# A three-stage kernel (attention, expert layer, dense layer): q with exchanged halves by TensorE and VectorE, not by DMA; two small operations on other engines

## The chip, the cores and the metric

The program runs on one core of one Trainium2 chip. The metric is the device time in microseconds from one launch to the end. Three runs of the kernel before gave 1102.35, 1104.45 and 1104.64 us, median 1104.45. A core has TensorE (PE; its weight loads stand apart as PEld), VectorE (DVE), ScalarE (ACT), GpSimd (POOL) and SyncE (SP), which issues most of the DMAs; 16 DMA engines move the data.

## The reference

Attention with a threshold on 4 batches x 8 heads, 576 positions, width 64; its output feeds a layer of 8 experts (top 1), and that a dense layer with `h - tanh(h)`. All in float32. Only the attention bears on the change:

```python
scores = scale * np.matmul(q, k.transpose(0, 1, 3, 2))
thresh = np.max(scores, axis=-1, keepdims=True) - tau
scores = np.where(scores >= thresh, scores, -1000000000.0)
scores = scores - np.max(scores, axis=-1, keepdims=True)
attn = np.exp(scores)
attn = attn / (np.sum(attn, axis=-1, keepdims=True) + 1e-09)
return np.matmul(attn, v).astype(np.float32)
```

## The kernel before

The attention is cut into 16 units. A unit is one head of two batches (`j` = 0, 1), and its 1152 rows of q are worked off in nine steps `t` of 128 rows; step 4 takes 64 rows of each batch. Partitions 0 to 63 and 64 to 127 hold the two halves of a float32 split: of q and k the rounded part (`hi`, by ScalarE, `split_hi`) and the rest (`lo`, `split_lo`), put side by side in the tile `x2`, transposed by TensorE (`tr`: the pieces `q0`, `m`, `q4`, `k0`, `k5`) into the one PSUM tile with the tag `t`, and written from there to SBUF (`evac`). So `QA` ("qa", 128 x 1280, of which 1216 columns are used) has q's rounded part on the partitions of one half and its rest on the other. The scores need all four products of parts, and get them as two products of full depth: `QA` with `ka`, and `QB` ("qb") with `ka`, where `QB` is `QA` with the two halves of its partitions exchanged. Two DMAs per unit make it (`swap`, L192 to L195), issued by SP.

What a step then does, engine by engine: TensorE writes the scores to PSUM (`scores`, L213, three buffers); VectorE takes the negative maximum (`smax`, L221); ScalarE the exponential (`sexp`, L227); VectorE masks, multiplies and sums (`smask`, L240, the sum into a column of `su`), and makes the next threshold (`sthr`, L231); ScalarE rounds the result to float16 (`split_e`, L248, tile `e16` with three buffers of three steps each); GpSimd makes the rest (`split_l`, L252 and L253). After three steps SP issues a DMA transpose of `e16` into `et` (`tr_e`, L259), and TensorE multiplies `et` by the two float16 parts of v (`pv`, L282). VectorE scales the products by the reciprocal `r` of the sums while it writes them to `x` (`pv_out`, L288). The reciprocal is made by `recip`: VectorE adds 1e-9 to `su` and multiplies it by v's scale `sc` (L267), then inverts it (L268). v itself is multiplied by its scale on VectorE (`v_w`, L137), rounded on ScalarE (`v_hi`, L141), and its rest is made on GpSimd (`v_lo`, L145). v's maximum (`v_max`, L123) is the first thing that uses a load of v (`load_v`, L103 to L105).

Each engine works off its instructions in the order in which the program is written. That order comes from a table: in `PL` each job has a pair (step, slot), relative to the first step of its unit; `PFIRST` and `PLAST` replace entries for the first and the last unit; `AFTER` lists which job has to stand ahead of which. `run` walks through the steps of all units: slot 0, the scores of the step after the next, slot 1, the maximum and exponential of the next step, the mask of this step, the next threshold, slots 2 and 3. A unit lasts nine steps, so the jobs of one unit's inputs lie among the steps of the unit before. After the last step come the routing to the experts, the expert layer and the dense layer; the change does not touch them.

The first unit's exchange is made in two pieces (`swap0` and `swap`).

Of the kernel before, what the change touches and what calls it, by code (L numbers as in the profile page):

```python
# [11 lines left out]
F32 = mybir.dt.float32  # L12
F32R = mybir.dt.float32r
# [4 lines left out]
AF = mybir.ActivationFunctionType  # L18
ALU = mybir.AluOpType
# [4 lines left out]
B, H, S, D = 4, 8, 576, 64  # L24
# [3 lines left out]
QS = S + 64  # L28


class Attn:
# [3 lines left out]
    def __init__(self, tc, ctx, q, k, v, tau, xtok, ident):  # L35
        self.tc, self.nc = tc, tc.nc
        self.q, self.k, self.v = q, k, v
        self.xtok, self.ident = xtok, ident
        nc = self.nc
        e = ctx.enter_context  # L40
        self.one = e(tc.tile_pool(name="a1", bufs=1))
        self.ld = e(tc.tile_pool(name="ald", bufs=2))
        self.wk = e(tc.tile_pool(name="awk", bufs=2))
        self.sp = e(tc.tile_pool(name="asp", bufs=3, space=PSUM))
        self.tp = e(tc.tile_pool(name="atp", bufs=1, space=PSUM))
        one = self.one
        self.raw, self.x2, self.vv, self.vs, self.vh, self.ka = {}, {}, {}, {}, {}, {}
        self.X, self.rr, self.rqk, self.tpu = {}, {}, {}, {}
        w = one.tile([128, 1], F32, name="warm")
        nc.vector.memset(w, 0.0)  # L50
        nc.scalar.activation(out=w, in_=w, func=AF.Exp)
        t = one.tile([128, 1], F32, name="tau")
        nc.gpsimd.dma_start(out=t, in_=tau.to_broadcast([128, 1]))
        self.load_qk(0, 0, 0, 1, nc.sync)
        self.load_qk(0, 1, 0, 1, nc.scalar)
        self.identr = one.tile([128, 128], F32R, name="identr")
        nc.vector.tensor_copy(self.identr, ident)
        self.g8 = one.tile([128, 1], F32, name="g8")
        nc.vector.tensor_scalar(out=self.g8, in0=t, scalar1=0.0, scalar2=0.125, op0=ALU.is_ge, op1=ALU.mult)
        self.ntau = one.tile([128, 1], F32, name="ntau")  # L60
        nc.vector.tensor_scalar(out=self.ntau, in0=t, scalar1=0.0, scalar2=-1.0, op0=ALU.max, op1=ALU.mult)
        z = one.tile([128, 64], F32, name="z64")
        nc.gpsimd.memset(z, 0.0)
        self.QA, self.QB = [], []
        for i in range(2):
            for lst, nm in ((self.QA, "qa"), (self.QB, "qb")):
                tl = one.tile([128, 2 * QS], F32R, name=f"{nm}{i}")
                nc.vector.tensor_copy(tl[:, S:S + 64], z)
                lst.append(tl)
        bank = self.tp.tile([128, 512], F32, name="ops")  # L70
        self.ops = bank[:, 0:6 * D].rearrange("p (a b d) -> p a b d", a=2, b=3)
        w = 6 * D + 9 * H
        self.lm = bank[:, 6 * D:w].rearrange("p (t e) -> p t e", t=9)
        self.vsum = bank[:, w:w + 4]
        self.c14 = one.tile([128, 128], F32, name="c14")
        nc.gpsimd.memset(self.c14, 2.0 ** -14)
        self.em, self.e16, self.et, self.sums = {}, {}, {}, {}
# [56 lines left out]
        V.reciprocal(out=sc, in_=pm)  # L134

    def v_w(self, u):
        self.nc.vector.tensor_scalar(out=self.vv[u], in0=self.vv[u], scalar1=self.vs[u][1], scalar2=None, op0=ALU.mult)  # L137

    def v_hi(self, u):
        self.vh[u] = self.wk.tile([128, 2, 2, 5, D], F16, tag="vh", name="vh", bufs=2)  # L140
# [51 lines left out]
    def swap(self, u, c0=0, c1=QS + S):  # L192
        a, bq = self.QA[u % 2].bitcast(F32), self.QB[u % 2].bitcast(F32)
        for o in (0, 64):
            self.nc.sync.dma_start(out=bq[o:o + 64, c0:c1], in_=a[64 - o:128 - o, c0:c1])  # L195


    def scores(self, u, t):
        nc = self.nc
        ps = self.sp.tile([128, 2, 512], F32, tag="s", name="sps")  # L200
        qa, qb, ka = self.QA[u % 2], self.QB[u % 2], self.ka[u]
        if t == 4:
            terms = [(j, 512 + 64 * j) for j in range(2)]
        elif t < 4:
            terms = [(0, 128 * t)]
        else:
            terms = [(1, QS + 64 + 128 * (t - 5))]
        n = len(terms) * 2
        i = 0
        for w in (qa, qb):  # L210
            for j, o in terms:
                for c in range(2):
                    nc.tensor.matmul(ps[:, c, 0:288], lhsT=w[:, o:o + 128], rhs=ka[:, j, 288 * c:288 * c + 288],  # L213
                                     start=(i == 0), stop=(i == n - 1))
                i += 1
        return ps
# [43 lines left out]
        self.et[u, g] = et  # L260


    def recip(self, u):
        nc = self.nc
        su = self.sums.pop(u)
        r = self.wk.tile([128, 9], F32, tag="r", name="r")
        nc.vector.tensor_scalar(out=su, in0=su, scalar1=1e-9, scalar2=self.vs[u][1], op0=ALU.add, op1=ALU.mult)  # L267
        nc.vector.reciprocal(out=r, in_=su)  # L268
        self.rr[u] = r

    def pv(self, u, t):
# [19 lines left out]
    def store(self, u):  # L291
        nc = self.nc
        P, h = divmod(u, H)
        if h % 2 == 1:
            c = slice((h - 1) * D, (h + 1) * D)
            X = self.X[u // 2]
            for j in range(2):
# [7 lines left out]
    PL = {"lq": (-21, 1), "lk": (-31, 2), "lv": (-12, 1), "hi0": (-16, 2), "hi1": (-15, 3), "lo0": (-13, 1),  # L305
# [6 lines left out]

    PFIRST = {"hi0": (-20, 2), "hi1": (-18, 0), "lo0": (-18, 0), "lo1": (-18, 1), "q0": (-17, 0), "eq0": (-16, 2),
# [6 lines left out]

    AFTER = ["lq hi0", "lk hi1", "hi0 lo0", "hi1 lo1", "lo0 q0", "lo0 q4", "lo0 m", "lo1 m", "lo1 k0", "lo1 k5", "q0 eq0",
             "eq0 m", "m em", "em q4", "q4 eq4", "eq4 k0", "k0 ek0", "ek0 k5", "k5 ek5", "eq0 swap", "em swap", "eq4 swap", "vm vn", "vn vc", "vc vw", "vw vh", "vh vl", "se sl", "sl te", "po2 st",
             "po0 t0", "po1 t1", "po2 t2", "t0 v0", "v0 t1", "t1 v1", "v1 t2", "t2 v2", "v0 l0", "v1 l1", "v2 l2", "l0 la", "l1 la", "l2 la"]

    def run(self, units, moe=None):
        nc = self.nc
# [3 lines left out]
        for x in self.AFTER:  # L330
            x, y = x.split()
            assert PL[x] < PL[y] or PL[x] == PL[y] and list(PL).index(x) < list(PL).index(y), (x, y)

        def at(b, job, f, *a):
            i, ph = PL[job]
            sched.setdefault((b + i, ph), []).append((f, a))

        for n, u in enumerate(units):
            b = 9 * n
            PL = {**self.PL, **(self.PFIRST if n == 0 else self.PLAST if n == NU - 1 else {})}  # L340
            if n % 4 == 0:
                e0 = 0 if n else 1
                at(b, "lq", self.load_qk, u // 4, 0, e0, 4)
                at(b, "lk", self.load_qk, u // 4, 1, e0, 4)
                at(b, "lv", self.load_v, u // 4)
                for e in range(4):
                    at(b + e, "vm", self.v_max, u + e)
                at(b, "vn", self.v_sum, u)
                at(b, "vc", self.v_scale, u)
            for i in range(2):  # L350
                at(b, f"hi{i}", self.split_hi, u, i)
            for i in range(2):
                at(b, f"lo{i}", self.split_lo, u, i)
            for w in ("q0", "m", "q4", "k0", "k5"):
                at(b, w, self.tr, u, w)
                at(b, "e" + w, self.evac, u, w)
            if n == 0:
                at(b, "swap0", self.swap, u, 0, 256)
            at(b, "swap", self.swap, u, 256 if n == 0 else 0)
            at(b, "vw", self.v_w, u)  # L360
            at(b, "vh", self.v_hi, u)
            at(b, "vl", self.v_lo, u)
            for t in range(9):
                at(b + t, "se", self.split_e, u, t)
                if n == NU - 1:
                    at(b + t, "se", self.split_l, u, t // 3, slice(t % 3, t % 3 + 1), nc.vector if t in self.LD else nc.gpsimd)
                elif t % 3:
                    at(b + t, "sl", self.split_l, u, t // 3, slice(2 * (t % 3 - 1), t % 3 + 1), nc.gpsimd)
                if t % 3 == 2:
                    at(b + t - 2, "te", self.tr_e, u, t // 3)  # L370
                at(b + t, "pv", self.pv, u, t)
            for g in range(3):
                at(b, f"po{g}", self.pv_out, u, g)
            at(b, "rc", self.recip, u)
            at(b, "st", self.store, u)
            if moe and u % 2 == 1:
                P, j = u // H, u % H // 2
                for g in range(3):
                    at(b, f"t{g}", moe.lg_tr, P, j, g)
                    at(b, f"v{g}", moe.lg_ev, P, j, g)  # L380
                    at(b, f"l{g}", moe.lg_mm, P, j, g)
                at(b, "la", moe.lg_add, P, j)
# [942 lines left out]
```

## Time and profile before

| | us |
|---|---|
| runs, median (lowest to highest) | 1104.45 (1102.35 to 1104.64) |
| the profiled execution | 1109.76 |
| its span, first to last instruction | 1108.1 |
| PE busy | 950.4 (86%) |
| DVE busy | 904.0 (82%) |
| POOL busy | 727.1 (66%) |
| ACT busy | 663.3 (60%) |

Busy times are of the whole span, and the stages differ: the attention lies between some 11 and 376 us after the start, the expert layer and the dense layer behind it. A share of DMA can pass 1, since a DMA engine can have more than one packet under way. A wait is written `engine what it was about to do <- who ended the wait`. A trailing `q` (SPq) is an engine's sequencer, which issues DMAs.

### The profile page before, as it was taken

Reading aid. Unit: us, or ns where it says so; the run is one execution under the profiler, and the core shown is the slowest. Engines: PE = TensorE matmul, PEld = TensorE weight load, DVE = VectorE, ACT = ScalarE, POOL = GpSimd, SP = SyncE. Lnnn points to the kernel's source line nnn. Section 1 sums busy time; section 2 is a strip of 40 time slices with the busy share of each in tenths; the row PEclk is TensorE's granted clock in tenths of the full one; section 3 lists DMA queues with packets and bytes.
Section 4 is the critical chain, followed back from the end, with each engine's and each line's share of the span. In section 5 each row is a group of like instructions: output and inputs, shape, how many; then the busy total and the mean of one; then the engine's idle time right before and its main releaser. Section 6 shows DMA issues by size and latency. Waiting matters only on the chain.

```text
span 1108.1 us, 20727 instructions
## 1 busy us (share of the span) xinstructions
PE 950.4 (86%) x7297; PEld 875.3 (79%) x7297; DVE 904.0 (82%) x1605; ACT 663.3 (60%) x1246; POOL 727.1 (66%) x629
## 2 busy tenths in 40 slices
PE   4687686875877557999999989899999999999997
PEld 3576675864766447989999989788999999999886
DVE  4898876966979449897789875998988989899894
ACT  5686776965887134444455546676566665656662
POOL 2886875865777236544466646887767767677673
PEclk9687886977898769899999999999999999999999
DMA  6899999999999766687888876420100101000000
GB/s 178 169 206 191 195 196 215 197 192 204 165 200 182 135 207 234 218 275 246 258 265 282 272 256 217 132 86 17 34 22 20 46 11 41 16 29 1 20 10 29
DMA packets 249769, 162.51 MB, mean 147 GB/s; under 512 B 180122, under 2 KB 222508, under 8 KB 249661
## 3 DMA queue, kind: packets, MB, share of 16 engines
q1 hardware_dynamic: 245901, 150.36, 57.1%
q0 software_dynamic: 3312, 10.49, 2.8%
q8 instruction: 59, 0.97, 0.4%
q14 instruction: 49, 0.40, 0.1%
q10 hardware_dynamic: 448, 0.30, 0.1%
HBM read 85.08 MB, written 23.60 MB: 98 GB/s over the span
## 4 chain that ended last, share of the span: by engine, by line
PE 46%; DVE 11%; issue 3%; DMA 2%; ACT 2%; POOL 1%; POOLq 0%; SPq 0%; DVEq 0%; ACTq 0%
PE h L1008 23%; PE y L1091 15%; PE y L1063 8%; DVE w L1204 2%; DVE w L1205 2%; DVE w L978 1%; DMA raw<-in_moe_w_dram 1%; DVE cv L1125 1%; DVE w L1202 1%; PE t L985 1%; DMA xr<-rows,idx 1%; ACT w L976 1%; DVE cm L1123 1%; DVE tm L1203 1%; DVE w L1206 1%
## 5 line engine op out<-in xcount | busy, mean ns | idle before, releaser
L252 POOL TENSOR_TENSOR e<-em,e 128x1024 f16<-128x1024 f32 (+1 forms) x98 | 158.3, 1615 | 88.2 <-ACT e L248 59.5
L1201 POOL TENSOR_SCALAR tm<-u 128x384 uint8<-128x384 f32 x88 | 128.7, 1463 | 50.5 <-ACT u L1197 49.9
L1008 PE MATMUL h<-xa,w 128*128 128x256 f32 (+6 forms) x864 | 139.8, 311 | 8.8 <-DVE hbuf L1044 6.6
L1063 PE MATMUL y<-hbuf,w 128*128 128x256 f32 (+6 forms) x864 | 139.8, 311 | 0.7 <-ACT yo L1066 0.7
L1008 PEld LDWEIGHTS h<-xa,w 128*128 128x128 f32 x864 | 129.8, 193 | 11.2 <-DVE hbuf L1044 7.7
L227 ACT ACTIVATE e<-sps,n 128x576 f32<-128x576 f32 x144 | 108.1, 751 | 49.8 <-DVE n L221 49.2
L240 DVE SCALAR_TENSOR_TENSOR em<-sps,n,e 128x576 f32<-128x576 f32 x144 | 116.5, 809 | 24.3 <-ACT e L227 17.3
L978 POOL TENSOR_TENSOR w<-raw,w 128x1024 fp32r<-128x1024 f32 x36 | 92.3, 2563 | 58.8 <-ACT w L976 38.7
L282 PE MATMUL ops<-vh,et 128*128 128x64 f16 (+1 forms) x2240 | 102.0, 206 | 32.5 <-DVE x L288 29.1
L1063 PEld LDWEIGHTS y<-hbuf,w 128*128 128x128 f32 x864 | 127.7, 191 | 1.4 <-ACT yo L1066 0.9
L221 DVE TENSOR_REDUCE n<-sps 128x1 f32<-128x576 f32 x144 | 107.1, 744 | 23.3 <-PE sps L213 23.2
L282 PEld LDWEIGHTS <-et 128*128 128x128 f16 (+1 forms) x2240 | 89.0, 111 | 44.8 <-issue 34.7
L1204 DVE SCALAR_TENSOR_TENSOR w<-y,w 128x384 f32<-128x384 f32 x96 | 123.7, 1289 | 0.0
L1197 ACT ACTIVATE u<-h 128x384 f32<-128x384 f32 x96 | 47.1, 491 | 118.6 <-PE h L1008 118.6
L248 ACT CAST e<-em 128x576 f16<-128x576 f32 x144 | 97.3, 677 | 31.6 <-DMA et<-e 30.3
L213 PE MATMUL sps<-ka,qa 128*128 128x288 f32 x320 | 91.3, 380 | 28.6 <-DVE em L240 23.2
L1008 PE MATMUL h<-xk,w 128*128 128x384 f32 x576 | 109.4, 337 | 2.0 <-DVE w L978 1.7
L1218 POOL TENSOR_TENSOR gl<-w,gh 128x384 fp32r<-128x384 f32 x83 | 85.2, 1027 | 38.8 <-ACT gh L1217 38.8
L1008 PEld LDWEIGHTS h<-xk,w 128*128 128x128 f32 x576 | 102.1, 188 | 6.7 <-DVE w L978 2.4
L1043 ACT ACTIVATE hbuf<-h 128x256 fp32r<-128x256 f32 (+6 forms) x72 | 31.1, 432 | 108.4 <-PE h L1008 108.3
L976 ACT CAST w<-raw 128x1024 fp32r<-128x1024 f32 x72 | 75.3, 1050 | 21.8 <-DVE poff L576 14.7
L1205 DVE SCALAR_TENSOR_TENSOR w<-y,w 128x384 f32<-128x384 f32 x96 | 77.3, 805 | 10.7 <-DVE w L1204 0.9
(224 smaller groups left out, 2264.7 us busy)
## 6 DMA issues: line engine op xcount, KB each, us to landing
raw<-in_moe_w_dram SPq DMA_DIRECT2D x64, 512.0 KB, 5.0
qb<-qa SPq DMA_DIRECT2D x30, 304.0 KB, 5.7
cv<-in_moe_w_in_dram SPq DMA_DIRECT2D x16, 512.0 KB, 6.3
cv<-in_moe_w_out_dram SPq DMA_DIRECT2D x16, 512.0 KB, 4.7
wscr<-cm SPq DMA_DIRECT2D x32, 256.0 KB, 2.4
raw<-wscr SPq DMA_DIRECT2D x16, 512.0 KB, 4.3
xw<-yT SPq DMA_DIRECT2D x24, 192.0 KB, 2.4
vv<-in_v_dram SPq DMA_DIRECT2D x8, 512.0 KB
```

Of the source, the lines that this page charges most:

```text
L221: nc.vector.tensor_reduce(out=n[:, 0:1], in_=ps[:, :, 0:288], axis=AX.XY, op=ALU.max, negate=True)
L227: nc.scalar.activation(out=e, in_=ps[:, :, 0:288], func=AF.Exp, bias=n[:, 0:1])
L240: nc.vector.scalar_tensor_tensor(out=self.em[u, g][:, i].rearrange("p (a b) -> p a b", a=2), in0=ps[:, :, 0:288], scalar=n[:, 1:2], in1=e, ...
L252: eng.tensor_tensor(out=e16[:, r, S + 64:], in0=em[:, r, 0:512], in1=e16[:, r, 0:512], op=ALU.subtract)
L282: nc.tensor.matmul(o[q], lhsT=et[:, base + c, q], rhs=vh[:, a, j, c if c < 5 else c - 5, :], start=(n == 0), stop=(n == len(terms) - 1))
L978: (self.nc.gpsimd if pool else self.nc.vector).tensor_tensor(out=l, in0=raw, in1=h.bitcast(F32), op=ALU.subtract)
L1008: self.nc.tensor.matmul(out, lhsT=a, rhs=b, start=(i == 0), stop=(i == len(parts) - 1))
L1063: nc.tensor.matmul(self.ys[d], lhsT=a[:, f % 2, s], rhs=b, start=(f == 0 and i == 0), stop=(f == 7 and i == 2))
L1091: nc.tensor.matmul(self.ys[m], lhsT=a[:, s], rhs=b[:, f % 2], start=(f == 0 and i == 0), stop=(f == 15 and i == 2))
L1201: nc.gpsimd.tensor_scalar(out=mk, in0=u, scalar1=RCUT * RCUT, scalar2=None, op0=ALU.is_gt)
L1204: V.scalar_tensor_tensor(out=w, in0=y, scalar=b, in1=w, op0=ALU.add, op1=ALU.mult)
L1205: V.scalar_tensor_tensor(out=w, in0=z, scalar=d, in1=w, op0=ALU.add, op1=ALU.mult)
```

## The change

From the second unit on, `QB` is no longer written by DMA. A constant 128 x 128 tile `flip` is the identity with its two column halves exchanged. `turn` multiplies it on TensorE with a third of `QA` (512, 512 and 192 columns) into the PSUM tile with the tag `t`, of which there is one buffer, shared with the transposes `tr` and with the expert layer's `lps`; `turned` copies that on VectorE to `QB`. The jobs are s0, x0, s1, x1, s2, x2 in this order. The first unit keeps its DMAs. Besides, the first half of `recip` becomes a job of its own on GpSimd (`denom`), four steps ahead of the rest, and `v_w` is an activation on ScalarE in place of the operation on VectorE. `PL` has seven new entries (a line of them is shown), `AFTER` the order "de rc", "em s0", "eq4 s0", and the chain s0 to x2.

```diff
         nc.vector.tensor_copy(self.identr, ident)
+        self.flip = one.tile([128, 128], F32R, name="flip")
+        for o in (0, 64):
+            nc.vector.tensor_copy(self.flip[:, o:o + 64], ident[:, 64 - o:128 - o])
...
     def v_w(self, u):
-        self.nc.vector.tensor_scalar(out=self.vv[u], in0=self.vv[u], scalar1=self.vs[u][1], scalar2=None, op0=ALU.mult)
+        self.nc.scalar.activation(out=self.vv[u], in_=self.vv[u], func=AF.Copy, scale=self.vs[u][1])
...
+    def turn(self, u, i):
+        self.tps = self.tp.tile([128, 4, 128], F32R, tag="t", name="tws")
+        a = self.QA[u % 2][:, 512 * i:min(512 * i + 512, QS + S)]
+        self.nc.tensor.matmul(self.tps.rearrange("p a b -> p (a b)")[:, 0:a.shape[1]].bitcast(F32), lhsT=self.flip, rhs=a,
+                              start=True, stop=True)
+
+    def turned(self, u, i):
+        b = self.QB[u % 2][:, 512 * i:min(512 * i + 512, QS + S)]
+        self.nc.vector.tensor_copy(b, self.tps.rearrange("p a b -> p (a b)")[:, 0:b.shape[1]].bitcast(F32))
...
+    def denom(self, u):
+        su = self.sums[u]
+        self.nc.gpsimd.tensor_scalar(out=su, in0=su, scalar1=1e-9, scalar2=self.vs[u][1], op0=ALU.add, op1=ALU.mult)
+
     def recip(self, u):
         nc = self.nc
-        su = self.sums.pop(u)
         r = self.wk.tile([128, 9], F32, tag="r", name="r")
-        nc.vector.tensor_scalar(out=su, in0=su, scalar1=1e-9, scalar2=self.vs[u][1], op0=ALU.add, op1=ALU.mult)
-        nc.vector.reciprocal(out=r, in_=su)
+        nc.vector.reciprocal(out=r, in_=self.sums.pop(u))
         self.rr[u] = r
...
+          "s0": (-7, 2), "x0": (-7, 3), "s1": (-6, 1), "x1": (-6, 2), "s2": (-6, 3), "x2": (-6, 3),
...
-            at(b, "swap", self.swap, u, 256 if n == 0 else 0)
+                at(b, "swap", self.swap, u, 256)
+            else:
+                for i in range(3):
+                    at(b, f"s{i}", self.turn, u, i)
+                    at(b, f"x{i}", self.turned, u, i)
...
+            at(b, "de", self.denom, u)
             at(b, "rc", self.recip, u)
```

What this makes of the order. First SP's queue in the middle of the attention, where `e_` tiles are `e16` and `raw` and `qb` the inputs; before:

```order
L259 DMA_TRANSPOSE et<-e_1621 128x27x128
L195 DMA qb_110<-qa_108 64x1216 x2
L259 DMA_TRANSPOSE et<-e_1749 128x27x128
L259 DMA_TRANSPOSE et<-e_1851 128x27x128
L90 DMA raw<-in_q_dram 64x4x576 x2
L259 DMA_TRANSPOSE et<-e_1956 128x27x128
L195 DMA qb_114<-qa_112 64x1216 x2
```

and now:

```order
L272 DMA_TRANSPOSE et<-e_1659 128x27x128
L272 DMA_TRANSPOSE et<-e_1787 128x27x128
L272 DMA_TRANSPOSE et<-e_1888 128x27x128
L93 DMA raw<-in_q_dram 64x4x576 x2
L272 DMA_TRANSPOSE et<-e_2001 128x27x128
```

The two exchange DMAs that stood behind the first of a unit's three transposes are gone, and nothing takes their place in this queue. Second VectorE, in the steps in which the inputs of the next unit are made (L288, now L303, is `pv_out`); before:

```order
L288 TENSOR_TENSOR x<-ops,r 128x3x64 x2
L221 TENSOR_REDUCE n<-sps 128x1
L240 SCALAR_TENSOR_TENSOR em,su<-sps,n,e 128x576
L231 TENSOR_SCALAR n<-n,ntau 128x1
L267 TENSOR_SCALAR su<-su,sc 128x9
L268 RECIPROCAL r<-su 128x9
L221 TENSOR_REDUCE n<-sps 128x1
L240 SCALAR_TENSOR_TENSOR em,su<-sps,n,e 128x576
L231 TENSOR_SCALAR n<-n,ntau 128x1
L137 TENSOR_SCALAR vv<-vv,sc 128x2x320
```

and now, from the same `pv_out` on:

```order
L303 TENSOR_TENSOR x<-ops,r 128x3x64 x2
L209 CAST qb_113<-tws 128x512
L234 TENSOR_REDUCE n<-sps 128x1
L253 SCALAR_TENSOR_TENSOR em,su<-sps,n,e 128x576
L244 TENSOR_SCALAR n<-n,ntau 128x1
L209 CAST qb_113<-tws 128x512
L209 CAST qb_113<-tws 128x192
L283 RECIPROCAL r<-su 128x9
```

The operations on `su` and on `vv` have left VectorE; three copies from the PSUM tile `tws` stand there instead, the second and the third with nothing between them. Third TensorE, where the transposes of k follow (`k0`, `k5`); before:

```order
L282 MATMUL ops<-vh,et 128x64
L164 MATMUL tps<-identr,x_1883 128x128 x4
L213 MATMUL sps<-ka,qa_108 128x288 x2
L213 MATMUL sps<-ka,qb_110 128x288 x2
L536 MATMUL ops<-wg,xT 128x8 x3
L164 MATMUL tps<-identr,x_1883 128x128 x4
```

and now:

```order
L297 MATMUL ops<-vh,et 128x64
L204 MATMUL tws<-qa_115,flip 128x192
L167 MATMUL tps<-identr,x_1922 128x128 x4
L226 MATMUL sps<-ka,qa_111 128x288 x2
L226 MATMUL sps<-ka,qb_113 128x288 x2
L557 MATMUL ops<-wg,xT 128x8 x3
L167 MATMUL tps<-identr,x_1922 128x128 x4
```

The last of the three products stands directly ahead of the transposes of k and of the scores, in the same PSUM tile as those transposes. On GpSimd the operation on `su` stands between the two parts of the last group's rests (L252, L253), ahead of the single step's.

## Rows read from the trace of the kernel before

**Rows 1.** The page's share of the DMA engines, in 40 slices of the span

```profile
DMA  6899999999999766687888876420100101000000
```

**Rows 2.** Busy time of each engine by stretch, clock, DMA share and rate

```profile
core 0: us, PE busy (x) PEld busy (x) DVE busy (x) ACT busy (x) POOL busy (x), PEclk, DMA share, GB/s
11.00:376.00 365.00, 267.32 (x3361) 241.95 (x3360) 287.60 (x723) 258.47 (x449) 258.03 (x286) 0.83 1.06 192
...
60.00:340.00 280.00, 206.86 (x2700) 189.53 (x2699) 226.61 (x566) 207.42 (x363) 202.65 (x192) 0.84 1.10 194
...
182.00:185.00 3.00, 2.64 (x22) 2.13 (x22) 2.97 (x5) 1.84 (x4) 2.58 (x3) 0.50 0.98 187
...
180.90:199.30 18.40, 14.68 (x171) 13.32 (x172) 18.00 (x43) 14.18 (x26) 12.09 (x12) 0.67 1.03 180
```

**Rows 3.** DMA in 60 to 340 us: packets, and the exchange's issues

```profile
DMA packets 150244, 54.40 MB, mean 194 GB/s; under 512 B 136184, under 2 KB 147064, under 8 KB 150210
...
qb<-qa SPq DMA_DIRECT2D x26, 304.0 KB, 5.7
```

**Rows 4.** Waits in 60 to 340 us: who waited for whom, total, times, longest

```profile
ACT e L248 <- DMA et<-e: 28.6, 12, 4.4
...
DVE em L240 <- ACT e L227: 17.3, 8, 4.1
...
DVE n L221 <- PE sps L213: 15.9, 24, 1.9
...
DVE pm L123 <- DMA vv<-in_v_dram: 12.9, 3, 4.7
...
PE sps L213 <- DMA qb<-qa: 0.4, 1, 0.4
```

**Rows 5.** Waits of SP's DMA queue in 60 to 340 us

```profile
SPq L259 <- POOL e L253: 83.4, 23, 7.4
```

**Rows 6.** Instructions in order of time: start, duration, engine, operation, idle before it

```profile
155.40 1.18 SPq L195 DMA_DIRECT2D qb<-qa  x2
156.69 11.85 SPq L259 DMA_TRANSPOSE et<-e  x2
...
167.00 0.67 ACT L248 CAST e<-em 128x576 f16<-128x576 f32 x1 [3.43 <-DMA et<-e]
...
168.98 0.82 DVE L240 SCALAR_TENSOR_TENSOR em<-sps,n,e 128x576 f32<-128x576 f32 x1 [2.99 <-ACT e L227]
...
179.46 0.82 DVE L123 TENSOR_REDUCE pm<-vv 128x1 f32<-128x640 f32 x1 [4.69 <-DMA vv<-in_v_dram]
...
198.76 0.42 POOL L253 TENSOR_TENSOR e<-em,e 128x128 f16<-128x128 f32 x1
...
202.49 1.33 DVE L267 TENSOR_SCALAR su<-su,sc 128x9 f32<-128x9 f32 x1
```

**Rows 7.** Groups by line and shape: count, busy us and mean ns of one

```profile
L1091 PE MATMUL y<-w,gh 128*128 128x512 f32 x258 | 81.1, 395 | 1.9 <-POOL w L978 1.1 <-ACT gh L1217 0.4 <-ACT yw L1066 0.3
...
L267 DVE TENSOR_SCALAR su<-su,sc 128x9 f32<-128x9 f32 x16 | 16.1, 1004 | 0.0
L288 DVE TENSOR_TENSOR x<-ops,r 128x192 f32<-128x192 f32 x48 | 15.4, 347 | 10.5 <-PE ops L282 10.5
L137 DVE TENSOR_SCALAR vv<-vv,sc 128x640 f32<-128x640 f32 x16 | 14.1, 882 | 0.0
...
L141 ACT CAST vh<-vv 128x640 f16<-128x640 f32 x16 | 11.6, 728 | 0.0
...
L188 DVE CAST ka<-two 128x512 fp32r<-128x512 f32 x1 | 0.7, 692 | 0.2 <-PE two L164 0.2
```

**Rows 8.** Single lines: durations in ns, lowest, median and highest

```profile
L137 DVE TENSOR_SCALAR vv<-vv,sc x16: 541/546/1818, 39.9 to 354.3; 128x640 f32<-128x640 f32 x16
...
L267 DVE TENSOR_SCALAR su<-su,sc x16: 227/1140/1658, 49.0 to 363.6; 128x9 f32<-128x9 f32 x16
...
L240 DVE SCALAR_TENSOR_TENSOR em<-sps,n,e x144: 800/808/820, 19.2 to 362.8; 128x576 f32<-128x576 f32 x144
```

More of the change, by code (lines that the diff above doesn't have):

```diff
@@ L322 @@
              "eq0 m", "m em", "em q4", "q4 eq4", "eq4 k0", "k0 ek0", "ek0 k5", "k5 ek5", "eq0 swap", "em swap", "eq4 swap", "vm vn", "vn vc", "vc vw", "vw vh", "vh vl", "se sl", "sl te", "po2 st",
-             "po0 t0", "po1 t1", "po2 t2", "t0 v0", "v0 t1", "t1 v1", "v1 t2", "t2 v2", "v0 l0", "v1 l1", "v2 l2", "l0 la", "l1 la", "l2 la"]
+             "po0 t0", "po1 t1", "po2 t2", "t0 v0", "v0 t1", "t1 v1", "v1 t2", "t2 v2", "v0 l0", "v1 l1", "v2 l2", "l0 la", "l1 la", "l2 la", "de rc", "em s0", "eq4 s0", "s0 x0", "x0 s1", "s1 x1", "x1 s2", "s2 x2"]
     def run(self, units, moe=None):
```

2 rows, old and new, of the table PL are left out of this document.

## The prediction

> **What bounds the kernel now.** I read the profile's slices first. The DMA engines are at nine tenths and over in most of the first third and nearly idle at the end [rows 1], so the stages have different limits. The change lies wholly in the attention; I take the stages after it as they are. From 11 to 376 us the DMA share is 1.06 [rows 2], above 1 because packets overlap. In the steady part, 60 to 340 us, it is 1.10, at 194 GB/s [rows 2]. That stretch holds 26 exchange DMAs [rows 3], two per unit, so 13 units, 280 / 13 = 21.5 us each. Per unit VectorE is busy 226.6 / 13 = 17.4 us, ScalarE 16.0, TensorE 15.9, GpSimd 15.6 [rows 2]. No engine fills the unit; DMA does.
>
> The waits tell how this reaches the engines. ScalarE waits 28.6 us for a transpose to free the float16 buffer, twelve times; VectorE 17.3 us for ScalarE; VectorE 12.9 us for v [rows 4]. In order of time one sees one such wait whole: the exchange's DMAs are issued at 155.40, the transposes behind them take SP 11.85 us for two, ScalarE's cast at 167.00 has waited 3.43 us for a transpose, and VectorE's mask at 168.98 another 2.99 us for ScalarE [rows 6]. The exchanged q itself is nearly never late (0.4 us, once) [rows 4]: it costs bandwidth, not latency.
>
> **The change part by part.** *DMA removed.* In 60 to 340 us the exchange carries 26 x 304 KB = 8.09 MB of 54.40 [rows 3], 14.9%. At the stretch's rate that is 0.149 x 280 = 41.6 us, 3.2 us a unit. A stretch that is nearly all exchange says the same: 0.623 MB a pair at 187 GB/s is 3.3 us [rows 2]. The unit's floor by DMA falls from 21.5 to 18.3 us. Fifteen units lose their exchange, the first keeps it: at most 15 x 3.2 = 48 us. SP also loses its two issues, 1.18 us a unit [rows 6]; what stood behind them is a transpose, which moves up.
>
> *VectorE.* Away go the scaling of v, 14.1 / 16 = 0.88 us, and the operation on the sums, 16.1 / 16 = 1.01 us [rows 7]. In come three copies out of PSUM. The row that fits is the 128x512 cast out of PSUM into the same type, 0.692 us [rows 7]; for 192 columns I take the 128x192 row, 0.347 us [rows 7]. Sum 1.73, net -0.16 us a unit.
>
> Both removed operations swing: 0.541 to 1.818 us for v's scaling, 0.227 to 1.658 us for 9 columns of sums, while the mask, L240, stays within 800 to 820 ns [rows 8]. So some 0.34 + 0.78 us of the two is waiting, inside the instruction. If it passes to another VectorE operation, the net is 1.73 - 0.54 - 0.23 = +0.96 us instead. I take -0.16, since the commonest operation that stays shows no such swing, and keep +0.96 in the range. The Trainium skill, SBUF — State Buffer, "Who interferes with whom", says VectorE and GpSimd share a port pair that is locked for a whole instruction, taken by VectorE's copies and scalings within SBUF, not by an operation with at most one input there. The mask's even row agrees; by that rule the waits leave with the two operations, and the sum is -0.16. Against the change speaks VectorE: DVE Perf Modes, "Mode 2×_2P": float32 scalings within SBUF run at double rate, reads out of PSUM do not. The trace agrees (640 columns in 546 ns, 512 out of PSUM in 692); by that alone the sum would be +0.96.
>
> *Added waits between TensorE and VectorE.* One PSUM buffer serves all three products, so each product waits for the copy before it. The first two hand-offs have a maximum and a mask (some 1.5 us) between them; nothing stands between the second copy and the third, so VectorE waits there for a whole product. No row shows this. Below, it is nothing, if VectorE has other waits in the same place. A 128x512 product takes 0.395 us at full clock [rows 7], 0.8 at 1.2 GHz (clock 0.50 occurs in this stage [rows 2]). If all five hand-offs are in series, they cost 3 x 0.4 + 1.73 = 2.9 us, of which the copies are counted: 1.2 us, 2.4 at half clock. Queued behind VectorE's wait is the reciprocal and the next maximum, for which ScalarE waits; behind TensorE's are the transposes of k and the next scores. In every second unit the first product also waits for ScalarE to empty the buffer of the router's transposes. I take 0.8 us, nearer to a product than to the series.
>
> *TensorE's* own work grows by at most 3 x 0.395 = 1.2 us a unit, 2.4 at half clock, on 15.9. *ScalarE* gets v's scaling: the row of its 640-column cast, 0.73 us [rows 7], on 16.0; the cast waited for this scaling anyway. *GpSimd* gets nine columns: above by its 128x128 row, 0.42 us, below by nothing. These three stay at or under 18.3 and are hidden by DMA and VectorE; uncovered they would cost up to 2.4, 0.7 and 0.4 us a unit. *The reciprocal* now waits for GpSimd. In the unit shown GpSimd has ended the operation ahead at 199.2 and VectorE comes to the sums at 202.49 [rows 6], 3.3 us of slack. Nothing; if it fails, the next maximum stands behind.
>
> *The sum.* What is late next is VectorE: 17.4 - 0.16 + 0.8. To that come waits that DMA does not cause: for the scores, 15.9 / 13 = 1.2 us; and half of v's waits, 12.9 / 13 / 2 = 0.5 us, since v's transfer is long itself and VectorE's arrival moves forward too. Together 19.75 us, over DMA's 18.3. The unit gets 1.75 us shorter, times 15 = 26 us. The profiled execution would go from 1109.76 (span 1108.1 and 1.7 around it) to 1084. The median of the runs is 5.3 us (0.5%) lower; taking 26 off it gives 1078.
>
> **The rivals.**
> *A: DMA sets the pace throughout.* All transfers stay dense and the whole 48 us come back: 1056. For it: the share of 1.10. Against it: SP waits 83.4 us of the 280 for GpSimd's float16 rests [rows 5], so the queue is not always fed; and from 180.9 to 199.3 VectorE is busy 18.0 of 18.4 us [rows 2], so it has no 3.2 us to give.
> *B: hidden anyway.* The chain VectorE, ScalarE, GpSimd, transpose sets the pace, and the time that the exchange gives back becomes idle DMA. For it: the same two rows. Against it: the 3.43 and 2.99 us waits right behind an exchange [rows 6]. Time: the net of VectorE, -0.16 to +0.96 a unit, with up to 0.5 us back from shorter waits: 1097 to 1112, about 1103.
> *C: slower, by the one PSUM buffer.* TensorE, in order, holds the scores back behind each copy; VectorE then waits for scores as well as products. Price: all hand-offs in series at half clock, 2.4 us a unit, plus one product that the scores wait for, 0.8, plus VectorE's +0.96. It decides from the point where this sum passes what DMA gives back, 3.2 us: 4.2 - 3.2 = 1.0 us a unit, 15 us: 1119. Against it: the first two hand-offs have other work between them, and the scores are made two steps ahead.
> That the change doesn't remove the DMAs is excluded: the transposes now stand next to each other in SP's queue.
>
> **How the numbers follow.** Chances: forecast 0.58, A 0.18, B 0.14, C 0.10. The forecast's own range is 1066 (no added waits: 0.8 us a unit, 12 us more) to 1095 (+0.96 in place of -0.16: 1.1 us a unit, 17 us less). The range of 8 in 10 takes in half of A and the better half of B: 1056 to 1101. Runs of this kernel lie 0.2% apart (2.3 us), so less than that is no change. Faster: 0.58 + 0.18 and 0.07 of B, 0.83. Same: 0.04, of B. Slower: 0.10 and 0.03 of B, 0.13.
>
> **What would show it.** Right: four exchange DMAs in the trace (the first unit's) where there were 34; ScalarE's wait for transposes well under 28.6 us in 13 units; units of 19 to 20 us; copies near 0.69 us; VectorE over 88% busy in the steady part, DMA share below 1.05. Waits of VectorE for products under 1 us a unit; L267's swing gone and L240 still within 800 to 820 ns. Wrong: the unit still at 21 us with idle DMA (B); waits of TensorE for the copies and of VectorE for the products above 2 us a unit (C); VectorE's other operations growing by the 1.1 us that the two removed ones waited; the reciprocal waiting for GpSimd.

## The result, and the profile after

The changed kernel takes 1079.89 us (median of 4 runs, 1077.72 to 1083.33), the kernel before 1103.84 us beside it (4 runs, 1102.35 to 1104.64). The ratio is 0.9776 with a 95% interval of 0.9752 to 0.9799: faster by 2.2%, 24 us. The forecast was 1078. The two profiled executions differ by more, 1109.76 against 1077.72, since the one of before lies above its other runs and the one of after is the lowest of its own.

The page after, with the span, the busy shares and the DMA slices (to hold against [rows 1]):

```profile
span 1075.6 us, 20756 instructions
...
PE 949.5 (88%) x7342; PEld 870.1 (81%) x7342; DVE 898.7 (84%) x1620; ACT 670.6 (62%) x1262; POOL 728.5 (68%) x645
...
DMA  6798999998989476786787976220100101000000
```

The attention is over about a slice sooner; the rest looks as it did. From the last mask (VectorE's operation that ends a step's work on the scores; L240 before, L253 after) to the end of the span it is 745.3 us before and 744.9 after, so all of the gain lies in the attention. Between the two profiled executions that is 32 us, between the medians 24, or 1.6 us for each of the fifteen units. In the steady part, which is 60 to 320 us here, the windows show (microseconds; busy time and count of each engine; TensorE's granted clock; DMA share; GB/s):

```profile
core 0: us, PE busy (x) PEld busy (x) DVE busy (x) ACT busy (x) POOL busy (x), PEclk, DMA share, GB/s
60.00:320.00 260.00, 213.65 (x2826) 190.50 (x2825) 230.71 (x600) 218.90 (x385) 211.65 (x212) 0.92 0.99 186
...
216.20:234.60 18.40, 16.99 (x223) 15.40 (x223) 16.71 (x46) 16.57 (x30) 15.41 (x15) 0.91 1.21 200
234.60:260.50 25.90, 17.87 (x212) 15.79 (x211) 20.24 (x52) 17.03 (x32) 16.93 (x18) 0.80 0.88 178
260.50:278.80 18.30, 16.90 (x224) 15.48 (x223) 16.56 (x45) 16.47 (x31) 15.56 (x15) 0.91 0.99 178
```

Against [rows 2] the DMA share falls from 1.10 to 0.99 and VectorE rises from 226.6 of 280 (81%) to 230.7 of 260 (89%). The lower three rows are three units in a row. Units 2 to 15, from first mask to first mask, take (315.1 - 41.1) / 14 = 19.6 us on average, before (346.2 - 42.6) / 14 = 21.7. They are of two kinds: the three that load v (the middle row is one) take 22.4 to 25.9 us, before 26.4 to 27.5; the other eleven 18.4 on average, before 20.2. In the plain unit of the last row VectorE is busy 16.6 of 18.3 us. TensorE's mean granted clock is higher too, 0.92 after against 0.84 in [rows 2].

The waits in 60 to 320 us (engine and line that waited, whom for; total, times, longest):

```profile
ACT e L240 <- DVE n L234: 24.7, 19, 7.0
...
PE tws L204 <- DVE qb L209: 20.9, 16, 5.8
...
DVE pm L126 <- DMA vv<-in_v_dram: 10.9, 3, 5.6
...
DVE qb L209 <- PE tws L204: 8.2, 16, 0.6
PE ops L297 <- DVE x L303: 7.2, 11, 0.9
...
DVE n L234 <- PE sps L226: 5.1, 12, 0.6
```

ScalarE's wait for the transposes, which led [rows 4], has no row any more. ScalarE and TensorE now wait for VectorE, and VectorE for v, for the products (L204, copied at L209) and, less than before, for the scores (L226). The groups of the added work (count | busy, mean ns | idle before):

```profile
L209 DVE CAST qb<-tws 128x512 fp32r<-128x512 f32 x30 | 20.5, 684 | 4.3 <-PE tws L204 4.2
...
L140 ACT ACTIVATE vv<-vv,sc 128x640 f32<-128x640 f32 x16 | 13.4, 836 | 0.0
...
L209 DVE CAST qb<-tws 128x192 fp32r<-128x192 f32 x15 | 5.3, 356 | 4.9 <-PE tws L204 4.9
L278 POOL TENSOR_SCALAR su<-su,sc 128x9 f32<-128x9 f32 x16 | 4.4, 274 | 1.6
```

### The profile page after: what moved, and what is told of

It reads as the page before. It is cut to its first block, busy times and chain, and to the rows that moved or that the text cites. A ratio compares the mean times of both kernels' runs of the same rounds, so it can differ in the third digit from the quotient of the medians.

```text
span 1075.6 us, 20756 instructions
## 1 busy us (share of the span) xinstructions
PE 949.5 (88%) x7342; PEld 870.1 (81%) x7342; DVE 898.7 (84%) x1620; ACT 670.6 (62%) x1262; POOL 728.5 (68%) x645
## 4 chain that ended last, share of the span: by engine, by line
PE 50%; DVE 8%; DMA 3%; issue 3%; ACT 1%; POOL 1%; POOLq 0%; DVEq 0%; SPq 0%; ACTq 0%; another core or an unknown queue 0%
PE h L1029 25%; PE y L1112 15%; PE y L1084 9%; DVE w L1225 2%; DVE w L1226 1%; DMA xr<-rows,idx 1%; PE t L1006 1%; DMA raw<-in_moe_w_dram 1%; DVE w L1223 1%; DVE cv L1146 1%; DVE w L999 1%; DVE tm L1224 1%; DVE w L1227 0%; DVE cm L1148 0%; ACT w L997 0%
## 5 line engine op out<-in xcount | busy, mean ns | idle before, releaser
L240 ACT ACTIVATE e<-sps,n 128x576 f32<-128x576 f32 x144 | 110.9, 770 | 33.1 <-DVE n L234 32.9
L253 DVE SCALAR_TENSOR_TENSOR em<-sps,n,e 128x576 f32<-128x576 f32 x144 | 116.7, 811 | 5.3 <-ACT e L240 3.4
L234 DVE TENSOR_REDUCE n<-sps 128x1 f32<-128x576 f32 x144 | 107.2, 744 | 10.6 <-PE sps L226 10.5
L297 PE MATMUL ops<-vh,et 128*128 128x64 f16 (+1 forms) x2240 | 95.8, 200 | 13.8 <-DVE x L303 12.9
L297 PEld LDWEIGHTS <-et 128*128 128x128 f16 (+1 forms) x2240 | 82.2, 106 | 25.8 <-issue 20.9
L261 ACT CAST e<-em 128x576 f16<-128x576 f32 x144 | 100.4, 698 | 2.0 <-DVE em L253 1.5
L226 PE MATMUL sps<-ka,qa 128*128 128x288 f32 x320 | 86.2, 362 | 9.4 <-DVE em L253 5.4
```

The costliest lines, as they stand in the source:

```text
L234: nc.vector.tensor_reduce(out=n[:, 0:1], in_=ps[:, :, 0:288], axis=AX.XY, op=ALU.max, negate=True)
L240: nc.scalar.activation(out=e, in_=ps[:, :, 0:288], func=AF.Exp, bias=n[:, 0:1])
L253: nc.vector.scalar_tensor_tensor(out=self.em[u, g][:, i].rearrange("p (a b) -> p a b", a=2), in0=ps[:, :, 0:288], scalar=n[:, 1:2], in1=e, ...
L261: self.nc.scalar.copy(self.e16[u, g][:, i, 0:S], self.em[u, g][:, i])
L297: nc.tensor.matmul(o[q], lhsT=et[:, base + c, q], rhs=vh[:, a, j, c if c < 5 else c - 5, :], start=(n == 0), stop=(n == len(terms) - 1))
```

## The experiments

Four runs took the change apart: the product alone, the two moves alone, and the change with the exchange's traffic or only its issues put back.

**The product alone.** The scaling of v and the operation on the sums go back to VectorE; the exchange stays on TensorE.

```diff
-        self.nc.scalar.activation(out=self.vv[u], in_=self.vv[u], func=AF.Copy, scale=self.vs[u][1])
+        self.nc.vector.tensor_scalar(out=self.vv[u], in0=self.vv[u], scalar1=self.vs[u][1], scalar2=None, op0=ALU.mult)
...
-        self.nc.gpsimd.tensor_scalar(out=su, in0=su, scalar1=1e-9, scalar2=self.vs[u][1], op0=ALU.add, op1=ALU.mult)
...
+        nc.vector.tensor_scalar(out=su, in0=su, scalar1=1e-9, scalar2=self.vs[u][1], op0=ALU.add, op1=ALU.mult)
```

> The exchange by product and copies, as in the changed kernel; v's scaling and the operation on the sums back on VectorE. Two limits (mine): with the exchange gone VectorE sets the pace, so its 1.9 us a unit of removed work come back nearly whole: 15 x 1.2 to 1.9 us = 18 to 28 us over the changed kernel, 1098 to 1108, about no gain over before. DMA alone: VectorE has slack, so 1080 as changed, at most 1085. VectorE's relief alone: copies added and nothing taken away, so slower than before, 1115 or more.

1099.0 us, ratio 0.994 (0.9914 to 0.9966): a quarter of the gain. The DMA share is down to 0.92, and VectorE, busy 236.7 of 260 us (91%), is the nearer limit:

```profile
60.00:320.00 260.00, 206.09 (x2649) 183.93 (x2648) 236.71 (x579) 200.54 (x350) 195.12 (x185) 0.90 0.92 173
```

**The moves alone.** The scaling on ScalarE and the sums on GpSimd, as in the change, with the exchange by DMA as before.

```diff
-                for i in range(3):
-                    at(b, f"s{i}", self.turn, u, i)
-                    at(b, f"x{i}", self.turned, u, i)
+                at(b, "swap", self.swap, u, 0)
```

> v's scaling on ScalarE and the operation on the sums on GpSimd, as in the changed kernel; the exchange by DMA as before. Two limits (mine): the DMA engines go on setting the pace, VectorE's 1.9 us a unit are mostly idle time: 1096 to 1104. DMA alone: 1104, no change. VectorE's relief alone: 15 x 1.9 = 28 us faster, 1076, or more, since no copies are added.

1104.18 us, ratio 0.9987 (0.9965 to 1.0009): no difference. VectorE is relieved, from 211.6 to 193.0 us in these 260, and DMA keeps the pace. ScalarE still waits for the transposes (25.0 us before in the same stretch), and VectorE's waits for ScalarE grow from 14.1 us, so its relief turns into waiting:

```profile
60.00:320.00 260.00, 190.06 (x2526) 174.53 (x2526) 192.97 (x508) 201.17 (x355) 195.57 (x195) 0.88 1.11 202
```

```profile
ACT e L261 <- DMA et<-e: 31.5, 18, 5.2
DVE em L253 <- ACT e L240: 27.7, 31, 3.1
```

**The exchange's transfers put back as ballast.** The changed kernel, and at the old place in SP's queue the two old DMAs of each unit, into a tile that nothing reads. The second version copies 16 columns in place of 1216: the same issues, nearly no bytes.

```diff
+    def spare(self, u, c0, c1):
+        a = self.QA[u % 2].bitcast(F32)
+        for o in (0, 64):
+            self.nc.sync.dma_start(out=self.QC[o:o + 64, c0:c1], in_=a[64 - o:128 - o, c0:c1])
...
+                at(b, "swap", self.spare, u, 0, QS + S)
```

> The changed kernel, and in its SP queue at the old place the exchange's two DMAs again, of the same size, into a tile that nothing reads. Two limits (mine): the bytes cost what they cost before, 2 to 3.2 us a unit that DMA falls behind: 1100 to 1110, all the gain gone. VectorE's relief alone: DMA was never the limit, 1080 as changed.

> As the run before, but the two DMAs carry 16 columns in place of 1216: the issues, their waits and their place in SP's queue, with a hundredth of the bytes. Two limits (mine): 1080 as changed, at most 1084. If SP's issue and order were what the exchange cost: as the run with all bytes, 1095 or more.

Full size: 1103.85 us, ratio 0.999 (0.9967 to 1.0012), the whole gain gone. Sixteen columns: 1084.06 us, 0.9794 (0.9753 to 0.9834), an interval that holds the changed kernel's ratio. So it is the bytes. With them back, the share is at 1.09 and ScalarE waits for transposes again:

```profile
60.00:320.00 260.00, 201.31 (x2559) 179.79 (x2559) 211.12 (x544) 200.80 (x353) 195.74 (x195) 0.87 1.09 200
```

```profile
ACT e L267 <- DMA et<-e: 12.6, 7, 4.0
```

These four shared 22 runs of the kernel before (median 1104.72). The next four tell what limits the changed kernel (before: 1106.01, 7 runs).

**More work for VectorE, more for TensorE.** The first copy of each unit made twice (0.68 us of VectorE); in another kernel the first product of each unit made three times.

```diff
-        self.nc.vector.tensor_copy(b, self.tps.rearrange("p a b -> p (a b)")[:, 0:b.shape[1]].bitcast(F32))
+        for _ in range(2 if i == 0 else 1):
+            self.nc.vector.tensor_copy(b, self.tps.rearrange("p a b -> p (a b)")[:, 0:b.shape[1]].bitcast(F32))
```

```diff
-        self.nc.tensor.matmul(self.tps.rearrange("p a b -> p (a b)")[:, 0:a.shape[1]].bitcast(F32), lhsT=self.flip, rhs=a,
-                              start=True, stop=True)
+        for _ in range(3 if i == 0 else 1):
+            self.nc.tensor.matmul(self.tps.rearrange("p a b -> p (a b)")[:, 0:a.shape[1]].bitcast(F32), lhsT=self.flip, rhs=a,
+                                  start=True, stop=True)
```

> The changed kernel with the first of the three copies made twice: 0.68 us of VectorE a unit more, 15 times, 10.2 us in all. VectorE bound (mine): 7 to 10 us slower than changed, 1087 to 1090. DMA bound: hidden, 1080 to 1083.

> The changed kernel with the first of the three products made three times into the same place: two more 512-column products a unit, 0.4 to 0.8 us, 15 times 6 to 12 us of TensorE. VectorE bound (mine): hidden, 1080 to 1083. TensorE or the one PSUM buffer as the limit (my rival C): 1086 to 1092.

The copy: 1088.58 us, 0.9849 (0.9827 to 0.9872). Against 0.9776 that is 0.7%, some 8 of the 15 x 0.68 = 10.2 us added, so VectorE is on the path in most units. The second copy also holds the PSUM buffer longer, but VectorE's waits for the products stay (8.3 us in 60 to 320 us, 8.2 without it), so that is not what costs. The products: 1082.73 us, 0.9793 (0.9767 to 0.9818), overlapping the changed kernel's interval: a longer first product is hidden. The third product, for which VectorE waits with nothing in between, was not lengthened.

**The maximum of v later.** VectorE meets v's transfer at L126 and waits 5.6 us with q's copies behind it, at the longest:

```profile
238.12 0.60 SPq L106 DMA_DIRECT2D vv<-in_v_dram  x1
238.13 0.40 PE L204 MATMUL tws<-qa,flip 128*128 128x512 f32 x1
...
244.76 0.82 DVE L126 TENSOR_REDUCE pm<-vv 128x1 f32<-128x640 f32 x1 [5.59 <-DMA vv<-in_v_dram]
245.50 0.68 DVE L209 CAST qb<-tws 128x512 fp32r<-128x512 f32 x1
246.24 0.80 PE L204 MATMUL tws<-qa,flip 128*128 128x512 f32 x1 [5.83 <-DVE qb L209]
246.96 0.74 ACT L240 ACTIVATE e<-sps,n 128x576 f32<-128x576 f32 x1 [6.97 <-DVE n L234]
```

TensorE stood idle with it, and its clock fell. The same 512-column product takes 0.40 us ahead of the wait and 0.80 us behind it; the granted clock is 1.00 (2.4 GHz) in the first of these stretches and 0.50 (1.2 GHz) in the second:

```profile
238.00:240.00 2.00, 1.30 (x21) 1.06 (x20) 1.18 (x5) 1.99 (x4) 1.90 (x4) 1.00 0.98 280
246.00:248.00 2.00, 1.57 (x15) 1.10 (x15) 2.00 (x6) 1.04 (x2) 0.00 (x0) 0.50 1.15 234
```

One line of the order puts v's maximum and what follows from it three steps later. It was run twice; another kernel had it together with the last copy on ScalarE (the second pair of lines).

```diff
-          "vm": (-7, 3), "vn": (-3, 1), "vc": (-3, 2), "vw": (4, 3), "vh": (5, 3), "vl": (6, 1),
+          "vm": (-4, 3), "vn": (0, 1), "vc": (0, 2), "vw": (4, 3), "vh": (5, 3), "vl": (6, 1),
...
-        self.nc.vector.tensor_copy(b, self.tps.rearrange("p a b -> p (a b)")[:, 0:b.shape[1]].bitcast(F32))
+        (self.nc.scalar.copy if i == 2 else self.nc.vector.tensor_copy)(b, self.tps.rearrange("p a b -> p (a b)")[:, 0:b.shape[1]].bitcast(F32))
```

> The changed kernel with v's maxima three steps later (some 6 us), so that VectorE does not wait for v's load; same instructions. VectorE bound (mine): its 10.9 us of waits for v in 260 us go, and with the three or four loads in the attention 8 to 12 us are gained: 1069 to 1074. DMA bound: v's load only shows that DMA is late; the wait moves to ScalarE's wait for transposes, 1077 to 1081.

> v's maxima three steps later once more, beside the changed kernel: if the 0.4% of the first time is real, 1074 to 1077 and 3 to 5 us under the changed kernel of this set; if DMA's floor holds in the units with loads, within 2 us of it.

> v's maxima later, and the last copy (192 columns) on ScalarE, so that VectorE neither makes it nor waits for its product: 0.35 us of work and up to 0.65 us of wait a unit, 15 times 5 to 15 us of VectorE. VectorE bound (mine): 5 to 12 us faster than with v's maxima later alone, 1060 to 1067, if ScalarE (84% busy) takes it. If DMA's floor of 18.3 us a unit binds first: 1066 to 1072, hardly faster than v's maxima later alone.

1077.45 us, 0.9736 (0.9704 to 0.9768), and the second time 1079.81 us, 0.976 (0.9733 to 0.9787), with the changed kernel at 0.9776 again beside it: no gain that can be told, and less than expected. VectorE's wait for v is gone; others stand in its place:

```profile
DVE qb L209 <- PE tws L204: 11.1, 19, 1.6
...
DVE em L253 <- issue: 8.3, 9, 4.9
...
ACT e L261 <- DMA et<-e: 7.2, 3, 5.2
```

Behind two of the three loads ScalarE now waits for a transpose instead (5.2 and 1.9 us), so DMA is late there with either order. It is not the limit of such a unit from end to end: in the one from 234.60 to 260.50 us above its share is 0.88. With the last copy on ScalarE as well: 1077.56 us, 0.9753 (0.9729 to 0.9777), again expected too low. Moving this copy does not pay:

```profile
60.00:320.00 260.00, 211.78 (x2890) 187.64 (x2890) 232.28 (x600) 228.35 (x406) 216.69 (x219) 0.96 1.02 190
```

```profile
DVE n L234 <- PE sps L226: 10.6, 21, 1.0
DVE em L253 <- ACT e L240: 6.6, 19, 1.8
...
DVE qb L209 <- PE tws L204: 3.0, 6, 0.6
```

VectorE waits 3.0 us for products in place of 11.1, but 10.6 for scores (6.2 with v's maxima later alone) and 6.6 for ScalarE (2.7), which is now 88% busy. Whether less work on VectorE would pay with nothing put on ScalarE is not shown.

**Each move undone by itself.** The product alone gave 6 us and the moves alone none, yet together they gave 24. Two kernels undo one move each (the lines of the first diff), beside the changed kernel once more (before: 1106.59, 7 runs).

> The changed kernel once more, beside the three others of this set: 1080, 0.9776 of before.

> The changed kernel with the operation on the sums back on VectorE. In the run with both operations back it took 0.47 us a unit there, v's scaling 1.70 us. VectorE bound (mine): 15 x 0.2 to 0.5 = 3 to 8 us slower than changed, 1083 to 1088. If the operation waits as long as in the kernel before (1.0 us): 1093 to 1096.

> The changed kernel with v's scaling back on VectorE. VectorE bound, and the wait inside the scaling as in the run with both back (1.70 us): 15 x 0.9 to 1.7 = 13 to 25 us slower, 1093 to 1105. If it costs its shortest time of 0.54 us alone: 8 us, 1088.

The changed kernel: 1080.45 us, 0.9776 (0.975 to 0.9803). Two waits of its second trace differ from those above:

```profile
DVE pm L126 <- DMA vv<-in_v_dram: 7.5, 3, 4.3
DVE n L234 <- PE sps L226: 6.8, 16, 0.6
```

Sums back on VectorE: 1082.21, 0.9782 (0.9752 to 0.9813). Scaling of v back: 1082.09, 0.9782 (0.9747 to 0.9817). Neither is told from the changed kernel; far more had been expected of the second. So the cost is in the pair, and the scaling of v shows where. Its lines by duration (lowest, median, highest), with both back and then alone:

```profile
L140 DVE TENSOR_SCALAR vv<-vv,sc x16: 541/1697/1708, 40.1 to 345.3; 128x640 f32<-128x640 f32 x16
```

```profile
L140 DVE TENSOR_SCALAR vv<-vv,sc x16: 546/870/1606, 40.6 to 326.4; 128x640 f32<-128x640 f32 x16
```

The order of time tells why. Before, with both back, and with v's alone (starts, durations):

```profile
205.46 0.54 DVE L137 TENSOR_SCALAR vv<-vv,sc 128x640 f32<-128x640 f32 x1
205.53 1.73 POOL L119 TENSOR_TENSOR x<-raw,x 128x576 fp32r<-128x576 f32 x1
```

```profile
158.14 1.42 POOL L122 TENSOR_TENSOR x<-raw,x 128x576 fp32r<-128x576 f32 x1
158.20 1.70 DVE L140 TENSOR_SCALAR vv<-vv,sc 128x640 f32<-128x640 f32 x1
```

```profile
210.90 3.03 POOL L122 TENSOR_TENSOR x<-raw,x 128x576 fp32r<-128x576 f32 x2
211.80 0.87 DVE L140 TENSOR_SCALAR vv<-vv,sc 128x640 f32<-128x640 f32 x1
```

Before, the scaling starts 0.05 to 0.08 us ahead of GpSimd's operation in 8 of 16 units, and takes 0.54 us there; in one other unit it starts 0.04 us ahead and takes 1.82. In the kernel with both back it starts 0.06 to 0.08 us behind the second of GpSimd's pair and ends 0.35 us after that ends, at 1.70 us, in 13 of 16 units. Alone on VectorE it starts, in the unit shown, 0.9 us behind the first of the pair and takes 0.87, and again it ends 0.35 us after that one. But for the unit at 0.04 us, that agrees with the Trainium skill, SBUF — State Buffer, "Who interferes with whom": whoever issues first has the shared ports for the whole instruction.

The 1.70 us then cost a second time, on TensorE. The product alone again, one unit on:

```profile
205.45 0.34 DVE L305 TENSOR_TENSOR x<-ops,r 128x192 f32<-128x192 f32 x1
...
205.85 0.57 PE L299 MATMUL ops<-vh,et 128*128 128x64 f16 x14 [2.55 <-DVE x L305]
...
207.06 1.52 PE L299 MATMUL ops<-vh,et 128*64 128x64 f16 x28
...
208.51 0.85 PE L226 MATMUL sps<-ka,qa 128*128 128x288 f32 x2
...
209.88 0.76 DVE L234 TENSOR_REDUCE n<-sps 128x1 f32<-128x576 f32 x1 [1.03 <-PE sps L226]
```

VectorE comes late to L305, which empties the PSUM tile of the product with v; TensorE waits 2.55 us for it with the scores queued behind; VectorE then waits 1.03 us for those scores. In 60 to 320 us TensorE waits for these copies 31.2 us with both back, 8.9 and 10.6 us with v's or the sums alone, 7.2 in the changed kernel; VectorE waits for scores 15.9, 6.6, 3.9 and 5.1 us. The last mask starts at 352.6 us with both back and at 330.6 in the changed kernel. Left open: why one operation back costs so little (10.4 us of sums or 14.5 us of v's scaling on VectorE over the whole kernel, 4 us at the last mask). A part fills idle time: VectorE's waits ahead of the mask (L253) in 60 to 320 us are 3.8 and 3.5 us in the two traces of the changed kernel, 1.5 with the sums back and none with v's scaling back. Its wait for v is 9.4 and 7.0 us in the two, not plainly different from the changed kernel's own (10.9 and 7.5). The rest has no place yet.

## Why the prediction was right

The sign, the size and the mechanism came out. Point by point:

- **DMA removed: shown; its 3.2 us a unit not by itself.** Four exchange DMAs are left, as foretold. Ballast of the same bytes costs the whole gain, and the issues without the bytes cost nothing measurable. How far the floor by DMA fell can't be read off, since VectorE holds the unit up before it is reached.
- **VectorE the next limit: shown for plain units, not for all.** The page has it at 89% busy in the steady part, and an added copy costs most of its length. In the three units with v's load late transfers still hold VectorE or ScalarE up, which the forecast, an average over units, did not separate.
- **Sum a unit.** 260 us are 260 / 19.57 = 13.3 units; the terms follow from the rows above. The last column is the second trace of the same kernel, in which VectorE is busy 231.2 us.

| term, us a unit | forecast | measured | again |
|---|---|---|---|
| VectorE's own work | 17.24 | 230.7 / 13.3 = 17.3 | 17.4 |
| waits for the products | 0.8 | 8.2 / 13.3 = 0.6 | 0.6 |
| waits for the scores | 1.2 | 5.1 / 13.3 = 0.4 | 0.5 |
| waits for v | 0.5 | 10.9 / 13.3 = 0.8 | 0.6 |
| sum | 19.75 | 19.2, unit 19.6 | 19.1, unit 19.6 |

- **VectorE's net of -0.16 us: right.** The copies took 0.684 and 0.356 us (0.692 and 0.347 taken from [rows 7]), and the waiting that sat inside the two removed operations left with them: the mask still takes 802 to 819 ns.
- **One term mis-sized, another left out, with opposite signs.** The wait for the scores was said to stay. In 60 to 320 us it is 14.2 us before, 12.8 with the exchange still on DMA, 15.9 with both operations still on VectorE, and 5.1 and 6.8 in the two traces of the changed kernel: it fell to less than half, with the exchange off DMA and at least one of the two operations moved (3.9 and 6.6 us with one of them back). TensorE's clock alone does not explain this, since it is 0.90 in the trace with 15.9 us and 0.90 in the one with 6.8. Other short waits of VectorE, 0.4 to 0.5 us a unit, were not in the sum. That the forecast came within 2 us of the measured time owes something to these two cancelling in part. The wait for v was said to halve, from 1.0 us a unit; at 0.8 and 0.6 it can't be told how far it fell.
- **The covers held.** ScalarE's scaling took 0.836 us (0.73 taken), GpSimd's sums 0.274 (0 to 0.42), and the first of TensorE's products cost nothing that can be told even trebled. The reciprocal waited once for GpSimd, 2.6 us in the last unit, but the stretch from the last mask to the end did not grow.
- **Rivals.** A (1056): no, the mean unit is 19.6 us and not 18.3, and added VectorE work shows. But the eleven plain units, at 18.4 us (18.7 in the second trace), lie near A's 18.3: there the two limits all but meet, and what tells them apart is that the second copy lengthens these units to 19.2 us. B (hidden anyway): no, by the ballast. C (the one PSUM buffer): no, waits for products are 0.6 us a unit, and a longer first product changes nothing that can be told. They stand where the prediction looked for them: 0.45 us at the third copy in most units, and 0.6 us at the first in every second unit.
- **Sums of the prediction that do not come out.** B's terms, -0.16 to +0.96 us with up to 0.5 back, times 15, give 1095 to 1119 and not 1097 to 1112. The chances that lie in the range of 8 in 10 add up to 0.74. Neither bears on the forecast.

What the forecast did not say is that its parts need each other: without the moves the product gave a quarter.

## What to carry to other kernels

When two limits lie close together, here DMA at 21.5 us a unit and VectorE at 17.4 busy plus its waits, a change that lifts one must not load the other: cost the parts together, since alone the one gave 6 us, the other nothing, and both 24. To tell bytes from issues on a busy queue, put the transfer back as ballast at full size and at a few columns. An operation whose duration swings with what GpSimd does beside it (here 0.54 to 1.82 us) has no one price, so look at what runs beside it before and after anything is moved ahead of it.

## What the runs showed of the hardware

The same 640-column scaling took 0.54 us where it began 0.05 to 0.08 us ahead of GpSimd's operation and 1.70 us where it began 0.06 to 0.08 us behind one, and with both operations back the schedule held it in the second place for 13 units in a row. Nine columns of sums took 0.29 to 3.13 us on VectorE with only that move undone, and 0.273 to 0.280 on GpSimd:

```profile
L284 DVE TENSOR_SCALAR su<-su,sc x16: 294/500/3134, 50.8 to 335.7; 128x9 f32<-128x9 f32 x16
```

```profile
L278 POOL TENSOR_SCALAR su<-su,sc x16: 273/274/280, 46.2 to 333.7; 128x9 f32<-128x9 f32 x16
```
